# Four settings of the planner that places array visits: entry at a chain's end with five free banks, two sums moved to VectorE, slack for the last inverses

## The chip, the cores and the metric

The kernel runs on one core of one Trainium2 chip. The time is device microseconds of one execution, from the first to the last instruction of that core and what lies around it. The kernel before was timed three times: 385.16, 385.24 and 385.40 us, median 385.24.

## The reference, cut to what matters

Two branches are computed from S = 2048 rows of D = 512 values and mixed by a gate.

```
x = A_q
g = sigmoid((x * gate_w).sum(-1, keepdims=True))
# branch A: a short convolution, a product, a long causal convolution of every channel
k_shift = sum_t k_pad[:, t:t+S, :] * shift_k[:, ks-1-t]      # ks = 4 taps
kv = k_shift * v
y  = irfft(rfft(kv, 2S) * rfft(ssm_k, 2S))[:S] + kv * ssm_D
a  = q * y
# branch B: dense layer, relu, dense layer (512 -> 1792 -> 512)
b  = maximum(x @ w1, 0) @ w2
return g * a + (1 - g) * b
```

All of it is float32. The transform of branch A is done as small matrix products, the dense layers as three products each of a high and a low part (high by high, high by low, low by high).

## The kernel before, in words

TensorE does two kinds of work. **Dense chains** are runs of 128x128 by 512 matmuls that add into one PSUM bank: a chain of the first layer (`mlp1`, lines 412 to 414) has 12 matmuls, a chain of the second (`mlp2`, lines 638 to 640) 15, or 12 in the third era, and a `product` of the last era (lines 496 to 498) 6. The 14 column blocks of the hidden layer are worked in three eras of 5, 5 and 4. In the third era the first layer is computed by a combination of matrix blocks that needs fewer products (`combine`): its tiles are called X, V and Y, and its operands are made by `minus` (line 446) on VectorE.

**Array visits** are runs of 32 small matmuls that use parts of the array side by side (64x32 or 32x64). They carry the convolution:

- `stage1` (line 683): the first step of the two forward transforms, tiles s1x and s1h, in the first 160 us.
- `conv_mid(g, ...)`: the spectral middle, in eight groups g = 0 to 7. Its visit consists of links that follow one another on TensorE: first the inverse of the group two before (`inverse`, line 876, tile iv, four banks), then two rounds f_h and two rounds f_x (line 796), each of two banks. Groups 0 and 1 have no inverse to begin with; two further calls, g = 8 and 9, hold nothing but the inverses of the groups 6 and 7.
- `conv_end` (line 970, tile cy): the last inverse step, four visits after 337 us.

Between the links of a group stands other work: ScalarE copies f_h out (`lower`, line 829, into ha) and the inverse out (line 886, into bv, from where it is stored to HBM as sb); VectorE makes the rest of ha (line 834) and five products with f_x read from PSUM (`mul`, line 842, into p, ha, qa and qb). Then eight additions of 128x512 (`sums`, line 848) fold these into p: the sums 0 and 1 from ha, 2 and 3 from qa, 4 and 5 from qb, 6 and 7 from ha again. GpSimd does them, except those that `DSUM` gives to VectorE: all eight of group 7, and 6 and 7 of group 6. In PSUM all of this shares eight banks with the dense chains (`"cv": 8`): a bank is given back when the engine that reads it has done so, ScalarE for hh, bv and y, VectorE for hl (lines 615 and 519), for y in the second era (line 648) and for f_x (line 842).

The order of every engine's instructions is written out by a planner (`Plan.order`) before the kernel is built. It knows each operation with an estimated duration, a rank, what it depends on and which banks and buffers it takes and gives; it walks through estimated time and starts on every engine the best-ranked operation that is ready. What it writes is a fixed order for each engine; on the chip an instruction then waits for what it needs, and everything behind it on its engine waits too. The planner lets only one of VectorE and GpSimd work on operations that it marks `port` at a time; on the chip nothing holds them apart.

Array links rank ahead of dense work (rank 0 against 1). Without a further rule a visit would start as soon as its operands are there. The rule is `need`: the head of a visit waits until that many of the eight banks are free, unless it has waited 20 us (`PATIENT`). `need` is 6 for the heads of the groups 0 to 7 (`NEEDM`), 4 for the two inverses alone and for `conv_end`. The planner looks at this after every dense operation, and a dense operation is three matmuls, a part of a chain: so a visit may stand within a chain. The flag `ends` marks the last operation of a chain. A dependence that comes from another engine is counted as met a little later than estimated (`SAFE`, 1.0 us for array links).

Of the kernel before, what the change touches and what calls it, by code (L numbers as in the profile page):

```python
# [13 lines left out]
S, D, DFF = 2048, 512, 1792  # L14
# [3 lines left out]
NJ = 32  # L18
# [64 lines left out]
class Plan:  # L83
# [2 lines left out]
    def __init__(self, room):  # L86
        self.room, self.ops, self.turn = dict(room), [], {}

    def add(self, eng, dur, rank, fn, deps=(), take=(), give=(), dma=0, fifo=(), tiles=False, port=False, alt=None, pair=0, soon=False, ends=False, need=0):
        rank = tuple(_flat(rank))  # L90
        op = dict(tiles=tiles, alt=alt, port=port or eng == "POOL" and not dma, eng=eng, dur=dur, rank=rank, fn=fn, take=tuple(take), give=tuple(give), dma=dma, fifo=tuple(fifo),
                  pair=pair, soon=soon, ends=ends or soon, need=need, wait=0, next=[], asked=0.0, n=len(self.ops), rest=(), member=False)
        op["fn"] = fn if alt is None else lambda: fn(op["eng"])
        for d in deps:
            if d is not None:
                d["next"].append(op)
                op["wait"] += 1
        for q in fifo:
            self.turn.setdefault(q, []).append(op["n"])
        self.ops.append(op)  # L100
        return op
# [6 lines left out]
    def order(self):  # L108
        now, seq, events = 0.0, 0, []
# [3 lines left out]
        left, last, out, mode, live, port, live_sums = sum(0 < o["pair"] < 3 for o in self.ops), None, [], False, [], 0.0, False  # L113
# [29 lines left out]
        while True:  # L143
            for eng, ops in ready.items():
                if busy.get(eng, 0.0) > now + 1e-9:
                    continue
                best, summing = None, busy.get("POOL", 0.0) > now + 1e-9 or any(not o["dma"] for o in ready.get("POOL", ()))
                if eng == "POOL":
                    ops = ops + [o for o in ready.get("DVE", ()) if o["alt"] and live_sums]
                late = [o for o in ready.get("DVE", ()) if o["port"] and not o["alt"] and o["asked"] < now - PATIENCE] if eng == "POOL" else ()  # L150
                for op in ops:
                    if eng == "DVE" and op["alt"] and summing and op["asked"] > now - SHARE:
                        continue
                    if op["port"] and (port > now + 1e-9 or late):
                        continue
                    if eng == "PE":
                        if live and op is not live[0]:
                            continue
                        if not live and op["member"]:
                            continue  # L160
                        if op["need"] and not live and op["asked"] > now - PATIENT and op["need"] > sum(o is None or o.get("over", False) for o in line["cv"]):
                            continue
                        if op["pair"] and not live and (left > KEEP or op["pair"] > 2) and op["asked"] > now - LONG[op["pair"] - 1] and not twin(op):
                            continue
                    if best is not None and op["rank"] >= best["rank"]:
                        continue
                    if any(len(line[t]) < op["take"].count(t) or any(o is not None and not o.get("over") for o in line[t][:op["take"].count(t)]) for t in op["take"]):
                        continue
                    if any(self.turn[q][0] != op["n"] for q in op["fifo"]):
                        continue  # L170
                    if op["dma"] and pipe > now + DMA_AHEAD:
                        continue
                    best = op
                if best is None:
                    continue
                op = best
                ready[op["eng"]].remove(op)
                if op["eng"] != eng:
                    op["eng"], op["dur"] = op["alt"]
                live_sums = live_sums or eng == "POOL" and not op["dma"]  # L180
                two = twin(op) if 0 < op["pair"] < 3 and not live else None
                if live and op is live[0]:
                    live.pop(0)
                if op["rest"]:
                    live = list(op["rest"])
                if two:
                    live = [two]
                if eng == "PE":
                    last = op
                    left -= 0 < op["pair"] < 3  # L190
                for t in op["take"]:
                    line[t].pop(0)
                for t in op["give"]:
                    line[t].append(op)
                for q in op["fifo"]:
                    self.turn[q].pop(0)
                op["start"] = now
                if op["port"]:
                    port = now + op["dur"]
                out.append(op)  # L200
                free = now + op["dur"]
                if eng == "PE":
                    if op["tiles"] != mode:
                        free += SWITCH
                    mode = op["tiles"]
                if eng == "PE" and now < PE_COLD:
                    free += op["dur"]
                done = free
                if op["dma"]:
                    pipe = max(pipe, free + DMA_LAG[0]) + op["dma"] / DMA_RATE  # L210
                    done = pipe + DMA_LAG[1]
                op["end"] = done
                busy[eng] = free
                event(free, "free", op)
                event(done + (0 if op["dma"] else LAG.get(eng, 0.0)), "done", op)
            if not events:
                break
            now = events[0][0]
            while events and events[0][0] <= now + 1e-9:
                _, _, what, op = heapq.heappop(events)  # L220
                if what == "wake":
                    continue
                if what == "go":
                    ask(op)
                    continue
                if what == "over":
                    op["over"] = True
                    continue
                if what == "done":
                    late = max([SLOW.get(t, 0) for t in op["give"]], default=0)  # L230
                    if late:
                        event(now + late, "over", op)
                    else:
                        op["over"] = True
                for o in op["next"]:
                    near = o["eng"] == op["eng"] and not op["dma"]
                    if near != (what == "free"):
                        continue
                    o["wait"] -= 1
                    if not o["wait"]:  # L240
                        s = 0 if near else SAFE.get(o["eng"] + str(int(o["rank"][0] != 0)) if o["eng"] == "PE" else o["eng"], 0)
                        if o["member"]:
                            s = 0
                        if o["eng"] == "PE" and not near and now < PE_START and o["rank"][0] == 0:
                            s += 1.5
                        if s:
                            event(now + s, "go", o)
                        else:
                            ask(o)
# [8 lines left out]
def dve_time(n):  # L258
    return n * 0.001042 + 0.12
# [8 lines left out]
def build(tc, wf, xp, qn, kn, vn, hn, dn, sh, gw, w1, w2, cs1, ccf, cci, cib, out):  # L268
# [19 lines left out]
    add = plan.add  # L288
# [490 lines left out]
    def conv_mid(g, gate):  # L779

        rank = (1, 500.0 + 4 * g)
# [2 lines left out]
        chain = []  # L784

        def link(dur, fn, deps, take, give=(), pair=0):
            o = add("PE", dur, (0, rank), fn, (deps if not chain else [chain[-1]]), take, give, tiles=True, pair=pair, need=0 if chain else NEEDM.get(g, 4))
            chain.append(o)
            return o

# [55 lines left out]
        def sums(dst, src, u, n, deps, sign=1, give=(), eng="POOL"):  # L846
            def go():
                (nc.gpsimd if eng == "POOL" else nc.vector).tensor_tensor(planes("p", dst, n), planes("p", dst, n), planes(src, u, n), op=OP.add if sign > 0 else OP.subtract)  # L848

            return add(eng, 0.11 + n * 1.14 if eng == "POOL" else dve_time(n * D), rank, go, deps, (), give, port=True)  # L850

        a = mul(0, 0, "p", 0, 0, 4, ha, give=["cv"], w=("p", 4))
        b = mul(1, 0, "ha", 2, 2, 2, [a])
# [207 lines left out]
DEBUG = None  # L1061
DIRECT = 3,
NEED, PATIENT = 4, 20.0
NEEDM = {g: 6 for g in range(8)}
NE = 4
XW = 512.0
PREP = 42.0, 43.0
SEED = [(2, c) for c in range(4)]
ALT = 0
DSUM = {7: tuple(range(8)), 6: (6, 7)}  # L1070
GATE = 690.0
EARLY = 2, 2
GN = 8
# [77 lines left out]
```

## Time and profile before

| what | value |
|---|---|
| median of three runs | 385.24 us |
| the profiled execution's own time | 384.69 us |
| its span, first to last instruction | 382.9 us |
| TensorE busy | 376.5 us, 98% |
| VectorE busy | 302.3 us, 79% |
| GpSimd busy | 79.1 us, 21% |
| granted TensorE clock | 1.0 throughout |

The profiled execution took 0.55 us less than the median of the others; 1.8 us of its time lie around the span. A matmul's busy time is modelled: dense matmuls are issued every 0.23 us and drawn 0.39 us long, so they overlap in the record, and a pause of TensorE is read from the chain of waits and from the starts, not from the busy sum. In the lists of instructions the first number is the start, the second the duration; in the groups the numbers after the bar are the busy time in us and the mean of one in ns.

### The profile page before, as it was taken

The numbers are of one execution on the slowest core, as the hardware profiler recorded it, in microseconds if no ns is written. First come the engines' busy times: TensorE is split into PE (matmuls) and PEld (weight loads), VectorE is DVE, ScalarE is ACT, GpSimd is POOL, SyncE is SP. The second block draws the span as 40 slices with busy tenths as digits, with TensorE's granted clock in tenths as the row PEclk, the third lists the DMA queues.
The fourth block names the chain that finished last, engine by engine and source line by source line (L and its number), as shares of the span: only waits on it lengthen the run. The fifth ranks groups of instructions, "written<-read, shape, count | busy, mean of one in ns | idle before, by whom it ended". The sixth has DMA issues, their size and how long they took to land.

```text
span 382.9 us, 6634 instructions
## 1 busy us (share of the span) xinstructions
PE 376.5 (98%) x2481; PEld 265.8 (69%) x2481; DVE 302.3 (79%) x389; ACT 169.9 (44%) x311; POOL 79.1 (21%) x63
## 2 busy tenths in 40 slices
PE   9999999999999999999999999999998999999996
PEld 5888866866866886786666465567485877866664
DVE  4699999699599863128868899668999998599863
ACT  5642366176256644523113513452346748464420
POOL 0000000000000000000995758989800000000000
PEclk9999999999999999999999999999999999999999
DMA  8998179777959969699669497899667733959823
GB/s 271 386 299 310 56 277 329 276 256 288 377 163 320 319 210 349 247 309 300 235 221 325 115 364 251 292 314 342 206 199 234 253 111 113 358 196 337 275 98 110
DMA packets 45523, 98.53 MB, mean 257 GB/s; under 512 B 4914, under 2 KB 7730, under 8 KB 45491
## 3 DMA queue, kind: packets, MB, share of 16 engines
q1 hardware_dynamic: 45202, 97.85, 74.4%
q8 instruction: 19, 0.31, 0.3%
q10 hardware_dynamic: 288, 0.26, 0.2%
q14 instruction: 14, 0.11, 0.1%
HBM read 67.68 MB, written 30.41 MB: 256 GB/s over the span
## 4 chain that ended last, share of the span: by engine, by line
PE 98%; DVE 1%; ACT 0%; DVEq 0%; issue 0%
PE m L638 14%; PE m L639 13%; PE m L640 13%; PE m L412 9%; PE m L413 9%; PE m L414 9%; PE iv L876 4%; PE f_h L796 4%; PE f_x L796 4%; PE m L398 3%; PE s1x L683 2%; PE cy L970 2%; PE X L496 2%; PE s1h L683 2%; PE X L497 2%; PE X L498 2%
## 5 line engine op out<-in xcount | busy, mean ns | idle before, releaser
L638 PE MATMUL m<-w1h_h,hh 128*128 128x512 f32 x224 | 89.0, 397 | 0.0
L639 PE MATMUL m<-w1l_l,hh 128*128 128x512 f32 x224 | 87.3, 390 | 0.0
L640 PE MATMUL m<-w1h_h,hl 128*128 128x512 f32 x224 | 87.2, 389 | 0.0
L848 POOL TENSOR_TENSOR p<-p,ha 128x512 f32<-128x512 f32 x26 | 34.0, 1325 | 196.8 <-DVE ha L842 196.3
L612 ACT ACTIVATE hh<-m 128x512 fp32r<-128x512 f32 x40 | 23.6, 599 | 80.6 <-PE m L414 79.8
L638 PEld LDWEIGHTS m<-w1h_h,hh 128*128 128x128 f32 x224 | 42.0, 188 | 20.7 <-ACT ev L688 6.5
L640 PEld LDWEIGHTS m<-w1h_h,hl 128*128 128x128 f32 x224 | 42.0, 188 | 9.0
L615 DVE SCALAR_TENSOR_TENSOR hl<-m,hh 128x512 fp32r<-128x512 f32 x40 | 27.3, 688 | 26.6 <-ACT hh L612 26.6
L639 PEld LDWEIGHTS m<-w1l_l,hh 128*128 128x128 f32 x224 | 42.1, 188 | 8.2
L412 PE MATMUL m<-xh_h,w0h_h 128*128 128x512 f32 x96 | 37.7, 393 | 0.0
L413 PE MATMUL m<-xl_l,w0h_h 128*128 128x512 f32 x96 | 37.4, 389 | 0.0
L414 PE MATMUL m<-xh_h,w0l_l 128*128 128x512 f32 x96 | 37.4, 389 | 0.0
L653 ACT COPY y<-m 128x512 f32<-128x512 f32 x28 | 16.5, 590 | 36.1 <-PE m L640 35.9
L742 DVE TENSOR_TENSOR acc<-acc,tmp 128x1024 f32<-128x1024 f32 x24 | 29.4, 1224 | 0.8
L886 ACT COPY bv<-iv 128x512 f32<-128x512 f32 x32 | 18.3, 598 | 18.7 <-PE iv L876 10.7
L412 PEld LDWEIGHTS m<-xh_h,w0h_h 128*128 128x128 f32 x96 | 18.0, 188 | 6.2 <-ACT bv L886 1.7
L739 DVE TENSOR_TENSOR tmp<-r,sht_sht 128x512 f32<-128x512 f32 x32 | 20.9, 685 | 0.1
L337 DVE TENSOR_TENSOR xl_l<-raw,xh_h 128x512 fp32r<-128x512 f32 x28 | 20.9, 792 | 0.0
L688 ACT COPY ev<-s1x 128x512 f32<-128x512 f32 x32 | 16.4, 600 | 9.7 <-PE s1x L683 9.7
L414 PEld LDWEIGHTS m<-xh_h,w0l_l 128*128 128x128 f32 x96 | 18.0, 188 | 3.8
L848 POOL TENSOR_TENSOR p<-p,qb 128x512 f32<-128x512 f32 x14 | 20.6, 1498 | 0.0
L413 PEld LDWEIGHTS m<-xl_l,w0h_h 128*128 128x128 f32 x96 | 18.0, 188 | 3.6
(149 smaller groups left out, 649.7 us busy)
## 6 DMA issues: line engine op xcount, KB each, us to landing
sa<-ev SPq DMA_DIRECT2D x64, 256.0 KB, 3.0
r_h<-sa SPq DMA_DIRECT2D x16, 512.0 KB, 6.0
r_x<-sa SPq DMA_DIRECT2D x16, 512.0 KB, 7.3
sb<-bv SPq DMA_DIRECT2D x32, 256.0 KB, 3.7
raw<-xp SPq DMA_DIRECT2D x28, 256.0 KB, 4.1
raw<-w SPq DMA_DIRECT2D x22, 256.0 KB, 4.0
r<-kn SPq DMA_DIRECT2D x10, 512.0 KB, 5.3
r<-hn SPq DMA_DIRECT2D x8, 512.0 KB, 4.4
```

Source lines behind the costliest of these rows:

```text
L337: (nc.gpsimd if eng == "POOL" else nc.vector).tensor_tensor(tile_of(lo, tag + "l", dt=F32R, bufs=bufs, p=p), T[key], T[hi].bitcast(F32), o ...
L412: mm(ps, part("h", f, k), T["x", "h", xe, c, k], start=k == 0, stop=False)
L413: mm(ps, part("h", f, k), T["x", "l", xe, c, k], start=False, stop=False)
L414: mm(ps, part("l", f, k), T["x", "h", xe, c, k], start=False, stop=k == 3)
L612: nc.scalar.activation(tile_of(("hh", era, c, f), "hh", dt=F32R, p=mp, bufs=HB), T["m1", era, c, f], AF.Relu)
L615: nc.vector.scalar_tensor_tensor(tile_of(("hl", era, c, f), "hl", dt=F32R, p=mp, bufs=HB), T["m1", era, c, f], 0.0, T["hh", era, c, f].bit ...
L638: mm(ps, T["hh", era, c, f][:, z], T["w", "h", 1, f], start=f == fs[0] and not seeding, stop=False, skip_group_check=True)
L639: mm(ps, T["hh", era, c, f][:, z], T["w", "l", 1, f], start=False, stop=False, skip_group_check=True)
L640: mm(ps, T["hl", era, c, f][:, z], T["w", "h", 1, f], start=False, stop=f == fs[-1], skip_group_check=True)
L742: nc.vector.tensor_tensor(T["acc", c], T["acc", c], T[dst], op=OP.add)
L796: mm(ps[b][32 * j:32 * j + 32, :], T[k("cf")][at, 64 * j + 32 * o:64 * j + 32 * o + 32], T[k("r", t, j // 2)][at, (j % 2) * D:(j % 2 + 1) ...
L848: (nc.gpsimd if eng == "POOL" else nc.vector).tensor_tensor(planes("p", dst, n), planes("p", dst, n), planes(src, u, n), op=OP.add if sign ...
```

## The change

Four things change in the planner's input and rules; no operation is added or taken away.

1. A visit's head (an operation with `need`, outside a running visit) starts only when the operation before it on TensorE was the last of a dense chain (`ends`) or itself an array link (`tiles`), unless it has waited 20 us. With this, `NEEDM` goes from 6 to 5 free banks. The first condition holds for `conv_end` too, whose `need` stays 4.
2. The sums 2 and 3 of group 6 (the seventh), the two from qa, go from GpSimd to VectorE.
3. A new delay `safe` of 2.5 us is added before the planner counts the inverses of the groups 6 and 7 as ready, when their last operand comes from another engine.
4. The planner's estimate for a sum on GpSimd goes from 1.25 to 1.30 us.

```
-    def add(self, eng, dur, rank, fn, ..., ends=False, need=0):
+    def add(self, eng, dur, rank, fn, ..., ends=False, need=0, safe=0):
...
                         if not live and op["member"]:
                             continue
+                        if op["need"] and not live and op["asked"] > now - PATIENT and last and not last["ends"] and not last["tiles"]:
+                            continue
                         if op["need"] and not live and op["asked"] > now - PATIENT and op["need"] > sum(o is None or o.get("over", False) for o in line["cv"]):
                             continue
...
+                        if not near:
+                            s += o["safe"]
                         if s:
                             event(now + s, "go", o)
...
-            o = add("PE", dur, (0, rank), fn, ..., need=0 if chain else NEEDM.get(g, 4))
+            o = add("PE", dur, (0, rank), fn, ..., need=0 if chain else NEEDM.get(g, 4), safe=IVSAFE if g >= NJ // 4 else 0)
...
-            return add(eng, 0.11 + n * 1.14 if eng == "POOL" else dve_time(n * D), rank, go, deps, (), give, port=True)
+            return add(eng, 0.16 + n * 1.14 if eng == "POOL" else dve_time(n * D), rank, go, deps, (), give, port=True)
...
-NEEDM = {g: 6 for g in range(8)}
+IVSAFE = 2.5
+NEEDM = {g: 5 for g in range(8)}
...
-DSUM = {7: tuple(range(8)), 6: (6, 7)}
+DSUM = {7: tuple(range(8)), 6: (2, 3, 6, 7)}
```

More of the change, by code (lines that the diff above doesn't have):

```diff
@@ L87, in __init__, with add @@
         self.room, self.ops, self.turn = dict(room), [], {}
-    def add(self, eng, dur, rank, fn, deps=(), take=(), give=(), dma=0, fifo=(), tiles=False, port=False, alt=None, pair=0, soon=False, ends=False, need=0):
+    def add(self, eng, dur, rank, fn, deps=(), take=(), give=(), dma=0, fifo=(), tiles=False, port=False, alt=None, pair=0, soon=False, ends=False, need=0, safe=0):
         rank = tuple(_flat(rank))
         op = dict(tiles=tiles, alt=alt, port=port or eng == "POOL" and not dma, eng=eng, dur=dur, rank=rank, fn=fn, take=tuple(take), give=tuple(give), dma=dma, fifo=tuple(fifo),
-                  pair=pair, soon=soon, ends=ends or soon, need=need, wait=0, next=[], asked=0.0, n=len(self.ops), rest=(), member=False)
+                  pair=pair, soon=soon, ends=ends or soon, need=need, safe=safe, wait=0, next=[], asked=0.0, n=len(self.ops), rest=(), member=False)
         op["fn"] = fn if alt is None else lambda: fn(op["eng"])
@@ L786, in link @@
         def link(dur, fn, deps, take, give=(), pair=0):
-            o = add("PE", dur, (0, rank), fn, (deps if not chain else [chain[-1]]), take, give, tiles=True, pair=pair, need=0 if chain else NEEDM.get(g, 4))
+            o = add("PE", dur, (0, rank), fn, (deps if not chain else [chain[-1]]), take, give, tiles=True, pair=pair, need=0 if chain else NEEDM.get(g, 4), safe=IVSAFE if g >= NJ // 4 else 0)
             chain.append(o)
```

## The prediction

> **What bounds the kernel now.** I read the page first: which engine is full, and who is on the chain that ended last.
>
> ```profile
> span 382.9 us, 6634 instructions
> ...
> PE 376.5 (98%) x2481; PEld 265.8 (69%) x2481; DVE 302.3 (79%) x389; ACT 169.9 (44%) x311; POOL 79.1 (21%) x63
> ...
> PE 98%; DVE 1%; ACT 0%; DVEq 0%; issue 0%
> ```
>
> TensorE (PE) is the bound from end to end. The change removes no matmul, so it can only win where TensorE pauses, or lose by new pauses. So the second view is the chain of waits in order of time, read visit by visit (start, duration), and the third the timeline of TensorE around the one long pause.
>
> ```profile
> 197.84 1.90 PE iv L876 x32
> 199.75 1.88 PE f_h L796 x32
> 201.62 1.99 PE f_x L796 x32
> ...
> 212.68 1.90 PE iv L876 x32
> ...
> 216.46 2.01 PE f_x L796 x32
> ...
> 227.54 1.90 PE iv L876 x32
> ...
> 231.32 1.99 PE f_x L796 x32
> ...
> 241.01 1.90 PE iv L876 x32
> 242.91 1.88 PE f_h L796 x32
> 244.79 1.72 PE f_x L796 x32
> ...
> 258.67 1.72 PE f_x L796 x32
> ...
> 272.55 1.99 PE f_x L796 x32
> ```
>
> Six visits hold an inverse and a forward part. iv and f_h always take 1.90 and 1.88 us; f_x takes 1.72 in two of them (groups 5 and 6) and about 1.99 in four (groups 2, 3, 4 and 7). These four pauses are 0.27 + 0.29 + 0.27 + 0.27 = 1.10 us.
>
> ```profile
> 289.33 0.39 PE L498 MATMUL X<-xh_h_t,w0l_l_s 128*128 128x512 f32 x1
> 291.54 1.98 PE L876 MATMUL iv<-p,cc 32*64 32x512 f32 x32 [1.82 <-DVE hl L519]
> ```
>
> The inverse of group 6, alone in its visit, stands 1.82 us for VectorE's hl of tile V: it lacks a PSUM bank, not its operand. The groups of waits name no other long one for TensorE's matmuls; what is left is 2.9 us that can be won, 0.8%.
>
> **Why these pauses are there.** First the f_x. I counted the dense matmuls between visits (groups by line, in the windows ahead of the visits of groups 2, 4, 5 and 7).
>
> ```profile
> L412 PE MATMUL m<-xh_h,w0h_h 128*128 128x512 f32 x7 | 2.7, 389 | 0.0
> ...
> L638 PE MATMUL m<-w1h_h,hh 128*128 128x512 f32 x13 | 5.2, 398 | 0.0
> ...
> L412 PE MATMUL m<-xh_h,w0h_h 128*128 128x512 f32 x4 | 1.6, 389 | 0.0
> ...
> L638 PE MATMUL m<-w1h_h,hh 128*128 128x512 f32 x8 | 3.1, 389 | 0.0
> ```
>
> A first-layer chain is four such triples, a second-layer chain five. Ahead of group 2 stand 7 = 4 + 3 triples, ahead of group 4 13 = 5 + 5 + 3, ahead of group 7 8 = 5 + 3: these visits cut a chain open, and all three pause. Group 5 stands after 4, a whole chain, and does not. The open chain keeps its bank through the visit; seven are left for 4 + 4 + 4, so the last f_x round waits for a copy on ScalarE one place further back. Group 3 pauses though it starts at a chain's end; there the queue of ScalarE is the reason:
>
> ```profile
> 213.21 2.17 ACT L334 CAST xh_h<-raw 128x512 fp32r<-128x512 f32 x4
> 215.28 0.58 ACT L886 COPY bv<-iv 128x512 f32<-128x512 f32 x1
> ...
> 229.54 1.07 ACT L886 COPY bv<-iv 128x512 f32<-128x512 f32 x2 [3.55 <-PE iv L876]
> ```
>
> Four casts stand ahead of the first bv, which starts 0.7 us after iv has ended at 214.58 (212.68 + 1.90); behind group 4's iv (227.54 + 1.90) it starts after 0.1.
>
> Then the 1.82 us, from the timelines of VectorE and GpSimd before it.
>
> ```profile
> 269.02 8.18 DVE L446 TENSOR_TENSOR r_b<-r_b,r_b 128x1024 f32<-128x1024 f32 x4
> ...
> 284.16 1.89 DVE L848 TENSOR_TENSOR p<-p,ha 128x512 f32<-128x512 f32 x3
> ...
> 290.71 0.69 DVE L519 SCALAR_TENSOR_TENSOR hl<-V,hh 128x512 fp32r<-128x512 f32 x1
> ```
>
> ```profile
> 268.15 3.51 POOL L848 TENSOR_TENSOR p<-p,qa 128x512 f32<-128x512 f32 x2
> 271.62 4.49 POOL L848 TENSOR_TENSOR p<-p,qb 128x512 f32<-128x512 f32 x2
> ```
>
> ```profile
> L446 DVE TENSOR_TENSOR ha<-ha,ha x2: 1224/1225/1226, 325.1 to 326.3; 128x1024 f32<-128x1024 f32 x2
> ...
> L848 POOL TENSOR_TENSOR p<-p,ha x26: 1284/1297/1730, 182.1 to 266.9; 128x512 f32<-128x512 f32 x26
> ...
> L848 DVE TENSOR_TENSOR p<-p,ha x6: 683/686/689, 284.2 to 305.1; 128x512 f32<-128x512 f32 x6
> ```
>
> Alone, an L446 takes 1.22 us; four would be 4.9. Here they take 8.18: 3.3 us lost while GpSimd's four sums of group 6 run (8.0 us instead of 4 x 1.30 = 5.2). That makes VectorE late for all that follows, hl among it: with 3.3 us less, hl would have been done before the bank was wanted at 289.6. The operand was not late: group 6's own last sum is the second of the three at 284.16, done by 285.4, 4.2 us ahead.
>
> **The change part by part.**
>
> *Entry at a chain's end.* The just ended chain's bank is released within the visit, as in groups 5 and 6. Three cuts healed: 3 x 0.27 = -0.82 us. If copies or casts are in the way, as in group 3, nothing is won there: 0 to -1.10 with group 3. I add half of group 3's, since a visit that moves off the era's last chain leaves the four casts behind: -0.96. For `conv_end` the last visit, at 369 us, moves by at most a few triples; its cover is VectorE's idle time ahead of the last but one output:
>
> ```profile
> 376.42 0.75 DVE L899 SCALAR_TENSOR_TENSOR r<-m,gs_gs,r 128x512 f32<-128x512 f32 x1 [1.75 <-PE m L640]
> ```
>
> VectorE waits 1.75 us there, so a visit two triples later (2 x 3 x 0.23 = 1.4 us) costs nothing; without that cover the tail would grow by up to the shift, one chain's rest of three triples, 2.1 us.
>
> *Five banks instead of six.* Visits may come one chain end earlier than before (group 2 at 195.8 in place of 197.84, by 9 x 0.227 = 2.04 us; likewise groups 4 and 7). TensorE gains nothing by that itself, but the work of VectorE and GpSimd that hangs on a visit starts earlier, and VectorE has room for it in some stretches and none in others (busy time by windows, DVE the third sum):
>
> ```profile
> 192.00:206.00 14.00, 14.00 (x133) 7.96 (x132) 9.64 (x10) 4.33 (x8) 10.35 (x9) 1.00 0.73 238
> 206.00:220.00 14.00, 14.00 (x133) 8.00 (x132) 12.65 (x14) 6.78 (x13) 10.84 (x8) 1.00 0.62 206
> 220.00:235.00 15.00, 15.00 (x138) 8.74 (x137) 14.69 (x14) 4.36 (x8) 10.46 (x8) 1.00 0.91 330
> 235.00:248.00 13.00, 13.00 (x130) 7.65 (x129) 9.62 (x11) 4.21 (x8) 11.22 (x10) 1.00 0.83 266
> 248.00:262.00 14.00, 14.00 (x134) 8.49 (x133) 10.35 (x11) 6.43 (x12) 12.40 (x11) 1.00 0.90 304
> ...
> 276.00:292.00 16.00, 14.18 (x70) 11.31 (x76) 15.90 (x21) 7.30 (x13) 0.11 (x1) 1.00 0.72 225
> ```
>
> The price: one more bank is still in VectorE's hands when the visit begins. iv takes four, f_h needs the fifth and a sixth after 1.90 us and the rest after 2.8. A VectorE that is later than planned by more than that stops TensorE inside the visit. How late it gets in a collision is shown by the splits at 214 us:
>
> ```profile
> 213.95 5.51 DVE L337 TENSOR_TENSOR xl_l<-raw,xh_h 128x512 fp32r<-128x512 f32 x4
> ```
>
> Four splits alone are 4 x 0.69 = 2.8 us, so 2.7 were lost to the two GpSimd sums beside them. A five-bank visit straight behind that pays 2.7 - 1.9 = 0.8; behind the 3.3 of 269 us, 1.4. No such visit is in this trace, so the cost lies between 0 and, for two such hits, 2.2; a shift of the collisions themselves could even save some of it. I take +0.6, nearer to none, because the one inverse that paid did so after the larger collision only.
>
> *Two sums to VectorE.* VectorE gets 2 x 0.686 = 1.37 us more; GpSimd loses 2 x 1.30 = 2.6. Two of the four colliding sums are gone, so I halve the 3.3: VectorE's account is 1.37 - 1.65 = -0.3. Ends: +1.37, if the remaining two still hold all four L446 up, and 1.37 - 3.3 = -1.9, if group 6 comes earlier and nothing collides.
>
> *Slack and estimate.* 2.5 us on an operand that was there 4.2 us early, for a visit that waits for banks: by itself 0. The estimate, 0.05 us for each sum, makes GpSimd's order truer (1.30 measured): 0.
>
> *The pause of 1.82.* VectorE is better off by 0.3 from the sums and by up to 2.04 from group 7's earlier entry: 2.3 against 1.82. That it all arrives is not sure, since VectorE is full from 269 to 292, so I leave 0.3: -1.5.
>
> The sum, against the profiled execution: 384.69 - 0.96 + 0.6 - 1.5 = 382.8 us. The runs' median lies 0.55 above that execution: **383.4 us**.
>
> The Trainium skill bears on the sums. "SBUF — State Buffer", section "SBUF: two separate sides", says that VectorE (with two SBUF inputs) and GpSimd share one pair of ports under an exclusive lock, held for a whole instruction. The stretched L446 and sums above agree in kind. By that rule each sum taken away frees its whole 1.30 us for VectorE, an account of 1.37 - 2.6 = -1.2 in place of my -0.3; the 0.3 us left of the pause would go too: 383.1. Against it speaks "Perfetto Trace Analysis", section "Optimizing Scalar/DVE Operations": moving work between these two might not help because of that port. That is the condition of the first rival below.
>
> **The rivals.**
>
> *The pause stays.* The bank, not the operand, was late, and neither the slack nor the two sums touch a bank. If VectorE's account comes out at +1.37, hl is as late as before even with the earlier visit. Then only the f_x are won, less the new waits: 385.24 - 0.96 + 0.6 = 384.9. For it speaks VectorE's full stretch; against it, that the loss of 3.3 has one visible cause, which shrinks.
>
> *Slower: visits that start too early.* With five banks f_h meets VectorE inside its late stretches at 214 to 219 and 269 to 277. From a lateness of 1.9 us on it decides. Two hits cost 0.8 + 1.4 = 2.2, the pause of 1.82 stays and grows with the extra 1.37 on VectorE, the f_x are won: 385.24 + 2.2 + 1.37 - 0.96 = 387.9 at the worst; with the hit at 269 alone and half of the 1.37, 385.24 + 1.4 + 0.7 - 0.96 = 386.4. For it: the windows at 12.65 of 14 and 14.69 of 15. Against: one visit of six stood behind such a collision before, and waited for ScalarE only.
>
> *All of it goes.* Every pause vanishes and no new one comes: 385.24 - 2.9 = 382.3. A floor: every visit keeps its entry and exit.
>
> **How the numbers follow.** A measurement of this kernel can tell 0.2%, 0.77 us, from no change: 384.47 to 386.01. Forecast with its own spread (382.6 to 384.4) 0.45, all gone 0.13, the pause stays 0.22, slower 0.20. The first two give faster, 0.58; the third lies at 384.9, same, 0.22; the fourth 0.20. The range runs from 382.0 (the floor less 0.3 for the runs' spread) to 386.7, which takes in the slower case but for its worst.
>
> **What would show it.** f_x at 1.72 us in all eight groups confirms the entry at the chain's end; 1.99 in a visit behind a whole chain refutes it. A count of triples ahead of each visit that is a sum of whole chains confirms that the rule acts. The wait of iv for hl gone from TensorE's waits, and the four L446 below 8.18 us, confirm the sums. A new wait of f_h for VectorE, or visits that are not earlier, would prove the five banks wrong. A dense chain that pauses for hl or xl would be a cause that I have not priced, and the forecast would fail by it.

## The result, and the profile after

| what | before | after |
|---|---|---|
| median, lowest and highest of the runs taken side by side | 385.22 us (384.71 to 385.40) | 382.72 us (382.37 to 384.35) |
| profiled execution, its own time | 384.69 us | 382.90 us |
| its span | 382.9 us | 381.1 us |

The ratio is 0.9942, interval 0.9924 to 0.9960: the changed kernel is faster by 0.6%. The granted TensorE clock was 0.998 to 1.0 in every run whose clock is on record here, but for six of the twelve runs of "the change with six banks" below, which show 0.995 to 0.996 and took 386.18 to 387.01 us where the other six took 384.24 to 384.70. Lines behind the change have moved down by 4: L876 is now L880 (iv), L796 is L800 (f_h, f_x), L446 is L450 (`minus`), L848 is L852 (the sums), L519 is L523 (hl of X, V, Y), L638 to L640 are L642 to L644.

The page of the changed kernel, the lines that answer to the first ones of the prediction:

```profile
span 381.1 us, 6637 instructions
...
PE 376.0 (99%) x2481; PEld 266.3 (70%) x2481; DVE 296.5 (78%) x387; ACT 169.9 (45%) x311; POOL 79.4 (21%) x65
...
PE 95%; DVE 1%; DMA 1%; issue 0%; ACT 0%; DVEq 0%
```

TensorE still bounds the kernel and does the same 2481 matmuls. DVE is busy 5.8 us less, although it has two sums more: four splits have gone the other way, to GpSimd, and its other instructions are shorter. The largest group of splits shows it, before (L337) and after (L341):

```profile
L337 DVE TENSOR_TENSOR xl_l<-raw,xh_h 128x512 fp32r<-128x512 f32 x28 | 20.9, 792 | 0.0
```

```profile
L341 DVE TENSOR_TENSOR xl_l<-raw,xh_h 128x512 fp32r<-128x512 f32 x25 | 16.3, 695 | 0.4 <-ACT xh_h L338 0.3
```

A split of this group takes 695 ns in the mean where it took 792. Four of them stood at 214 us beside sums of GpSimd and took 5.51 us; that collision is gone. DMA has a share of the chain that it did not have; that is a new pause, shown below.

The chain of waits of the changed kernel, visit by visit (start, duration):

```profile
195.87 1.90 PE iv L880 x32
...
199.65 1.72 PE f_x L800 x32
...
213.53 1.72 PE f_x L800 x32
...
226.05 1.99 PE f_x L800 x32
...
270.01 1.72 PE f_x L800 x32
...
288.95 1.90 PE iv L880 x32
```

Three of the four f_x pauses are gone (groups 2, 3 and 7); group 4 still has its 0.27 us. The inverse of group 6 follows the dense matmul before it without a wait, 2.6 us earlier than before.

What VectorE did ahead of it, from its timeline:

```profile
263.73 0.68 DVE L852 TENSOR_TENSOR p<-p,qa 128x512 f32<-128x512 f32 x1
...
266.06 1.30 DVE L852 TENSOR_TENSOR p<-p,qa 128x512 f32<-128x512 f32 x1
...
267.88 5.19 DVE L450 TENSOR_TENSOR r_b<-r_b,r_b 128x1024 f32<-128x1024 f32 x3
...
274.19 1.21 DVE L450 TENSOR_TENSOR r_b<-r_b,r_b 128x1024 f32<-128x1024 f32 x1
...
288.13 0.68 DVE L523 SCALAR_TENSOR_TENSOR hl<-V,hh 128x512 fp32r<-128x512 f32 x1
```

and GpSimd beside it:

```profile
266.89 3.85 POOL L852 TENSOR_TENSOR p<-p,qb 128x512 f32<-128x512 f32 x2
```

The four L450 take 5.19 + 1.21 = 6.4 us, where they took 8.18. The last of them ends at 275.4; before, they ended at 277.2. The hl of V that the inverse stood for begins at 288.13 and not at 290.71. The margin is thin: it is done at 288.8, and the inverse starts at 288.9.

One pause is new. The groups of waits name it, and the timeline of ScalarE shows why; the load's row is from the chain of waits:

```profile
PE m L642 <- ACT m L636: 0.6, 1, 0.6
```

```profile
307.67 1.14 ACT L338 CAST xh_h_b<-ha 128x512 fp32r<-128x512 f32 x2 [0.93 <-DMA ha<-xp]
308.72 0.58 ACT L636 COPY m<-y 128x512 f32<-128x512 f32 x1
```

```profile
302.71 4.94 DMA ha<-xp
```

In the third era a chain may begin from a partial sum that ScalarE copies into its bank (m<-y, the seed). In the kernel before, the seed stood ahead of two casts of a freshly loaded block:

```profile
309.30 0.59 ACT L632 COPY m<-y 128x512 f32<-128x512 f32 x1
309.82 1.14 ACT L334 CAST xh_h_b<-ha 128x512 fp32r<-128x512 f32 x2
```

Now it stands behind them, and the casts stand for the load, which lands 4.94 us after its issue. TensorE starts the seeded chain 0.73 us late by the starts of its matmuls.

**Where the time went.** From the first spectral visit to the last dense matmul, by these rows of the chain and the timeline of before, and of after:

```profile
174.48 1.88 PE f_h L796 x32
...
378.71 0.39 PE L640 MATMUL m<-w1h_h,hl 128*128 128x512 f32 x1
```

```profile
175.23 1.88 PE f_h L800 x32
...
376.92 0.39 PE L644 MATMUL m<-w1h_h,hl 128*128 128x512 f32 x1
```

That is 378.71 - 174.48 = 204.23 us before, less 0.68 because the visit now has one triple more ahead of it, so 203.55; and 376.92 - 175.23 = 201.69 after: 1.86 us less. The pauses account for it: -0.82 (three f_x), -1.89 (the inverse, by starts; 1.82 in its row), +0.73 (the seed), together -1.98; the 0.1 us that is left lies behind the seed's pause, where the second matmul of the chain starts 0.34 us after the first (309.36 and 309.69) and dense matmuls otherwise follow at 0.23. The medians differ by 2.5 us. The profiled execution of before lay 0.5 us below its median, that of after 0.2 above; what lies ahead of 175 us varies from one execution to the next: the same changed kernel, profiled again for the last table, had this visit at 175.93.

### The profile page after: what moved, and what is told of

It is laid out like the page before. It is cut to its first block, busy times and chain, and to the rows that moved or that the text cites. A ratio compares the mean times of both kernels' runs of the same rounds, so it can differ in the third digit from the quotient of the medians.

```text
span 381.1 us, 6637 instructions
## 1 busy us (share of the span) xinstructions
PE 376.0 (99%) x2481; PEld 266.3 (70%) x2481; DVE 296.5 (78%) x387; ACT 169.9 (45%) x311; POOL 79.4 (21%) x65
## 4 chain that ended last, share of the span: by engine, by line
PE 95%; DVE 1%; DMA 1%; issue 0%; ACT 0%; DVEq 0%
PE m L642 13%; PE m L644 13%; PE m L643 13%; PE m L416 9%; PE m L417 9%; PE m L418 9%; PE iv L880 4%; PE f_h L800 4%; PE f_x L800 4%; PE m L402 3%; PE s1x L687 2%; PE cy L974 2%; PE X L500 2%; PE s1h L687 2%; PE X L502 2%; PE X L501 2%
## 5 line engine op out<-in xcount | busy, mean ns | idle before, releaser
L642 PE MATMUL m<-w1h_h,hh 128*128 128x512 f32 x224 | 89.0, 397 | 0.6 <-ACT m L636 0.6
L644 PE MATMUL m<-w1h_h,hl 128*128 128x512 f32 x224 | 87.2, 390 | 0.0
L852 POOL TENSOR_TENSOR p<-p,ha 128x512 f32<-128x512 f32 x26 | 33.7, 1312 | 190.5 <-DVE ha L846 190.1
L642 PEld LDWEIGHTS m<-w1h_h,hh 128*128 128x128 f32 x224 | 42.0, 188 | 20.8 <-ACT ev L692 6.5
L644 PEld LDWEIGHTS m<-w1h_h,hl 128*128 128x128 f32 x224 | 42.0, 188 | 9.0
L838 DVE TENSOR_TENSOR ha<-f_h,ha 128x512 f32<-128x512 f32 x16 | 10.6, 689 | 14.0 <-PE f_h L800 13.8
L652 DVE TENSOR_TENSOR y<-m,y 128x512 f32<-128x512 f32 x16 | 10.9, 682 | 12.7 <-PE m L644 12.7
```

The source lines that it names most:

```text
L642: mm(ps, T["hh", era, c, f][:, z], T["w", "h", 1, f], start=f == fs[0] and not seeding, stop=False, skip_group_check=True)
L644: mm(ps, T["hl", era, c, f][:, z], T["w", "h", 1, f], start=False, stop=f == fs[-1], skip_group_check=True)
```

## The experiments

Each ran beside the kernel before on the same chip, five rounds. Two questions: which of the four parts carries the gain, and whether the causes that the prediction named (a bank held by a cut chain; VectorE late because it collides with GpSimd) are the causes.

### The entry rule with five banks, alone

The kernel before, with

```
+   if op["need"] and not live and op["asked"] > now - PATIENT and last and not last["ends"] and not last["tiles"]:
+       continue
...
-NEEDM = {g: 6 for g in range(8)}
+NEEDM = {g: 5 for g in range(8)}
```

> The kernel before with entry at a chain's end and five free banks alone; the sums of group 6 stay on GpSimd, no slack. Theory (the cut chains cost the f_x, an earlier group 7 helps VectorE): f_x at 1.72 us in seven or eight groups, -0.8 to -1.1 us. The four sums still collide with the four L446 (about 8 us), but group 7 enters some 2 us earlier, so the wait of group 6's inverse shrinks from 1.8 to below 1: in all -1.7, 383.5 us. Rival (the two sums are what removes the inverse's wait): the wait stays at 1.5 to 1.9 and only the f_x are won, 384.3 us.

Measured: 382.59 us (382.25 to 384.00), before 385.28; ratio 0.9938 [0.9925, 0.9951]. Its chain of waits:

```profile
226.06 1.99 PE f_x L800 x32
...
270.69 1.99 PE f_x L800 x32
...
289.22 1.95 PE iv L880 x32
```

The whole gain is there without the sums. Two f_x pauses stay, and the inverse of group 6 loses 0.04 us, though the four L450 still take 7.4 us: they start earlier (266.56 against 269.02), since group 6's visit stands at 251.7 in place of 254.9 and VectorE is through with its products sooner.

### The entry rule with six banks, alone

As above, but with the number of before:

```
 NEEDM = {g: 6 for g in range(8)}
```

> The kernel before with entry at a chain's end, six free banks as before. Theory: the same f_x as with five banks, -0.8 to -1.1 us; visits come later than before instead of earlier, so VectorE is as late as before at hl of V and the inverse of group 6 waits 1 to 1.9 us: 384.2 us. Rival (five banks bring nothing, the chain's end does all): no difference from the run with five banks, 383.5 us.

Measured: 383.71 us (383.32 to 384.66), before 385.28; ratio 0.9968 [0.9959, 0.9978]: slower than with five banks by 1.1 us. From its waits, and its chain around 230 us:

```profile
PE f_h L800 <- DVE y L652: 0.6, 1, 0.6
PE iv L880 <- DVE hl L523: 0.4, 1, 0.4
```

```profile
228.88 2.65 DVE w0l_l L341 x2
...
232.19 1.09 PE f_h L800 x16
```

This is the wait that the prediction feared of five banks: f_h stands for a bank in VectorE's hands, since VectorE comes late out of a collision (two splits in 2.65 us instead of 1.28). It came with six, because the visit of group 4 had moved to 228.7, into the collision; with five it starts at 222.2. Of the 1 to 1.9 us expected at the inverse of group 6, 0.5 came; f_h lost 0.8 us instead.

### Five banks, alone

The kernel before, with

```
-NEEDM = {g: 6 for g in range(8)}
+NEEDM = {g: 5 for g in range(8)}
```

> The kernel before with five free banks, visits may still cut a chain open. Theory: five of the six visits now cut a chain (the order written out has them after 8, 10, 10, 11 and 21 triples), each pays 0.3 us or more in f_x, some pay in f_h as well since one bank less is free: f_x and f_h pauses of 1.5 to 3 us in place of 1.1, and the inverse of group 6 stands elsewhere (before the X products), without its 1.8: 384 to 386 us. Rival (earlier visits are good by themselves): below 383.6.

Measured: 383.41 us (383.13 to 383.51), before 385.28; ratio 0.9953 [0.9941, 0.9965]. Its visits again cut chains, five of six, and these five f_x pause; the sixth stands at a chain's end and does not. Groups 2 and 3 of its chain of waits:

```profile
199.34 1.99 PE f_x L798 x32
...
211.46 1.72 PE f_x L798 x32
...
279.53 1.90 PE iv L878 x32
```

Group 3 (nine triples of the first layer ahead: one that ends the cut chain, then two whole chains) runs in 1.72, group 2 (eight, a chain cut) in 1.99. The inverse of group 6 now starts at 279.5, within the second layer's work, and stands for nothing. So the time is that of the rival, below 383.6: the pause of 1.89 us is gone, and five cut chains cost 1.35.

### The two sums, alone

The kernel before, with

```
-DSUM = {7: tuple(range(8)), 6: (6, 7)}
+DSUM = {7: tuple(range(8)), 6: (2, 3, 6, 7)}
```

> The kernel before with the sums 2 and 3 of group 6 on VectorE alone. Theory of the prediction: two colliding GpSimd sums less, the four L446 take 6.5 us in place of 8.2, VectorE does 1.4 us more itself; the wait of group 6's inverse goes from 1.8 to about 1.5 or, if the lock rule holds in full, to 0.6; the f_x stay at 1.99 in four groups: 384.2 to 384.9 us. Rival (the sums alone remove the wait): wait below 0.2, 383.4 us. Rival (moving work between engines that share a port brings nothing): 385.2 us or more.

Measured: 383.28 us (382.88 to 383.96), before 385.28; ratio 0.9951 [0.9939, 0.9963]. VectorE's timeline:

```profile
271.50 3.73 DVE L448 TENSOR_TENSOR r_b<-r_b,r_b 128x1024 f32<-128x1024 f32 x3
...
276.35 1.22 DVE L448 TENSOR_TENSOR r_b<-r_b,r_b 128x1024 f32<-128x1024 f32 x1
```

4.95 us for the four: not half of their loss is gone but all of it, because the two sums left to GpSimd ran at 268.18 to 271.0, ahead of them. But now these meet the two sums that VectorE has taken over:

```profile
267.00 1.65 DVE L850 TENSOR_TENSOR p<-p,qa 128x512 f32<-128x512 f32 x1
...
270.30 1.28 DVE L850 TENSOR_TENSOR p<-p,qa 128x512 f32<-128x512 f32 x1
```

They take 2.93 us where two alone take 1.37, so about half of the collision is left, moved to other instructions. The hl of V starts 2.2 us earlier than before (288.55 against 290.71). About half of that is the collision; the other half is the planner's new order, which puts a product of group 7 (qb, at 292.15 where it was at 286.57) and one sum behind hl, and one split ahead of it. The inverse of group 6 has no pause, as the rival expected; the four f_x of before keep theirs.

### GpSimd held back, the orders as before

To show that the collision is the cause, the kernel before keeps every order, and GpSimd alone is made to wait for the last of the four L446: a tiny extra addition ahead of its sum 2 of group 6 reads one of their outputs.

In `sums`, ahead of the addition:

```
+                if g == 6 and eng == "POOL" and (src, u) == ("qa", 0):
+                    s = tile_of(("scr",), "scr", 8, p=mp)
+                    z = T["xc", 0, "t4"][:, :8]
+                    nc.gpsimd.tensor_tensor(s, z, z, op=OP.add)
```

> The kernel before, every engine's order unchanged, with one small addition of 128x8 on GpSimd ahead of group 6's first qa sum that reads what the last of the four L446 wrote: so GpSimd waits for them and nothing collides there. Theory (the collision makes VectorE late, its lateness makes hl and so the bank late): the four L446 take 4.9 us in place of 8.2, hl of V ends about 3 us earlier, the inverse of group 6 waits less than 0.3 us, the f_x pauses stay: 385.2 - 1.6 = 383.6 us. Rival (the bank is bound otherwise, for instance by ScalarE's hh of V): the wait stays above 1 us, 384.5 to 385.2 us. Rival (GpSimd's sums, now 5 us later, become the operand that is late): a wait for p, 385 us or more.

Measured: 383.17 us (382.81 to 383.74), before 384.96; ratio 0.9958 [0.9946, 0.9971]. GpSimd's timeline, then VectorE's:

```profile
274.44 0.20 POOL L851 TENSOR_TENSOR scr_scr<-r_b 128x8 f32<-128x8 f32 x1 [5.90 <-DVE r_b L446]
274.60 2.55 POOL L852 TENSOR_TENSOR p<-p,qa 128x512 f32<-128x512 f32 x2
277.10 2.55 POOL L852 TENSOR_TENSOR p<-p,qb 128x512 f32<-128x512 f32 x2
```

```profile
269.36 4.99 DVE L446 TENSOR_TENSOR r_b<-r_b,r_b 128x1024 f32<-128x1024 f32 x4
...
288.04 0.69 DVE L519 SCALAR_TENSOR_TENSOR hl<-V,hh 128x512 fp32r<-128x512 f32 x1
```

Nothing was moved off GpSimd, and it idles 5.9 us; the four L446 fall from 8.18 to 4.99 us, hl of V comes 2.7 us earlier, and the pause is gone. TensorE's order is that of the kernel before, matmul by matmul. So VectorE was late because of the collision, and the pause came from that lateness.

### The change without the two sums

The changed kernel, with

```
-DSUM = {7: tuple(range(8)), 6: (2, 3, 6, 7)}
+DSUM = {7: tuple(range(8)), 6: (6, 7)}
```

> The changed kernel with the sums 2 and 3 of group 6 back on GpSimd. Theory: the four L446 meet four sums again, about 8 us in place of 6.3, VectorE is 1 to 2 us later at hl of V, and since the inverse started with a margin of less than 0.1 us behind hl in the changed kernel, its wait comes back with 0.5 to 1.5 us: 383.2 to 384.2 us. Rival (the earlier entry alone has removed the wait): no wait, 382.7 us.

Measured: 383.11 us (382.70 to 384.28), before 384.96; ratio 0.9957 [0.9944, 0.9969]. GpSimd's four sums and the L450 collide as before (7.65 us), yet the inverse of group 6 loses only 0.08 us of the 0.5 to 1.5 expected. What the sums buy inside the change is small: the visit of group 7 pauses 0.57 us in this kernel and not at all in the changed one, and the chain with the seed starts 0.1 us late.

```profile
268.73 2.33 PE f_h L800 x31
```

Of the 0.57, 0.45 are f_h's, 2.33 us long where it is 1.88 in the changed kernel: it stands until 269.97 for a bank that VectorE gives back at 269.93 with its addition into y, late out of the collision. This is the wait that the prediction priced, with five banks; the rest is f_x behind an open chain.

### The change with six banks

The changed kernel, with

```
-NEEDM = {g: 5 for g in range(8)}
+NEEDM = {g: 6 for g in range(8)}
```

> The changed kernel with six free banks. Theory: the visits of groups 2 to 7 come a chain end later (the order written out has group 7 3.6 us later), f_x stays at 1.72 in seven or eight groups, the wait of group 6's inverse is between 0 and 1 us because its own place moves back too: 382.7 to 383.5 us. Rival (five banks are needed): 384 us or more.

Measured: 385.44 us (384.24 to 387.01, 12 runs), before 384.96; ratio 1.0013 [0.9997, 1.0029]. Not 382.7 to 383.5, but the rival's 384 or more. At a granted clock of 1.0 it took 384.24 to 384.70 us, so 0.4 us of the gain is left there; why the clock was lower in the other runs is not shown. A wait from its list, VectorE's timeline at that place, and GpSimd's:

```profile
PE m L642 <- DVE ha L838: 2.0, 1, 2.0
```

```profile
213.81 5.90 DVE L341 TENSOR_TENSOR xl_l<-raw,xh_h 128x512 fp32r<-128x512 f32 x4
```

```profile
212.82 2.98 POOL L852 TENSOR_TENSOR p<-p,qb 128x512 f32<-128x512 f32 x2
215.88 3.28 POOL L852 TENSOR_TENSOR p<-p,ha 128x512 f32<-128x512 f32 x2
```

Four splits that alone take 2.8 us take 5.90 beside four sums; behind them VectorE reads f_h late and gives its bank back late, and the dense chain after group 3's visit cannot begin. In the kernel before, the splits took 5.51 us there and VectorE read f_h hardly sooner (219.38, against 219.63), yet the chain behind that visit began without a wait, in a bank that ScalarE gave back. So it is the collision together with the order in which the banks are handed out that costs the 2 us. The profiled execution took 384.56 us.

### The seed ahead of the casts

The planner's estimate of the load is lengthened until its order puts the seed first; the orders of TensorE, GpSimd and SyncE stay.

In `combine` of the changed kernel:

```
-    raws[nm] = add("SP", ISSUE, -47, go, [...], [...], dma=2 * ROW)
+    raws[nm] = add("SP", ISSUE, -47, go, [...], [...], dma=2.3 * ROW)
```

> The changed kernel with the planner's estimate for four loads of the second combination raised by 15% of their size: this moves on ScalarE one copy (the seed of a bank from y) ahead of two casts that wait for a load, and leaves the order of TensorE, GpSimd and the queues as it is. Theory (the new pause of a dense chain, 0.73 us at 308 us, is the seed standing behind casts whose load lands late): the pause goes, 382.7 - 0.7 = 382.0 us. Rival (the bank of the seed is late anyway): the pause stays, 382.7 us.

Measured: 382.55 us (382.28 to 382.78), before 384.96; ratio 0.9937 [0.9926, 0.9949]. ScalarE's timeline:

```profile
306.96 0.60 ACT L636 COPY m<-y 128x512 f32<-128x512 f32 x1
308.28 1.14 ACT L338 CAST xh_h_b<-ha 128x512 fp32r<-128x512 f32 x2 [0.73 <-DMA ha<-xp]
```

The casts still stand for the load, and nobody stands for them; TensorE's new pause is gone from the profile. The times alone do not show it: 382.55 is nearer to the rival's 382.7 than to 382.0, and the ratio lies within the interval of the changed kernel's first measurement (0.9924 to 0.9960). Nor is the spread of the changed kernel (to 384.35) explained by the seed alone: the two sums alone, whose seed is ahead of the casts, spread from 382.88 to 383.96.

### No visit while a chain is open

Group 4 kept its pause although ten triples, two times five, stand ahead of it. The groups by line, from the end of group 3's visit to the start of group 4's in the changed kernel:

```profile
L642 PE MATMUL m<-w1h_h,hh 128*128 128x512 f32 x6 | 2.3, 389 | 0.0
...
L416 PE MATMUL m<-xh_h,w0h_h 128*128 128x512 f32 x4 | 1.7, 418 | 0.0
```

Four of the first layer, a whole chain, and six of the second: 5 + 1. (The entry rule with five banks alone has such a six ahead of group 4 and of group 7, the two whose f_x pauses there.) Two chains are interleaved there; the last operation before the visit ends one of them, and the other is open, its bank held. So this version of the last kernel counts open chains, one more when a dense operation takes a bank and one less at a chain's end:

```
-   if op["need"] and not live and op["asked"] > now - PATIENT and last and not last["ends"] and not last["tiles"]:
+   if op["need"] and not live and op["asked"] > now - PATIENT and last and (opened > 0 or not last["ends"] and not last["tiles"]):
...
+   if not op["tiles"] and op["rank"][0] == 1 and op["rank"][1] > 0:
+       opened += op["take"].count("cv") - op["ends"]
```

> The changed kernel with the seed moved ahead of the casts, as in the run before, and a stricter rule of entry: a visit starts only when no dense chain is open, not merely when the last operation ended one (group 4's visit entered while another chain, begun one triple before, was open; it moves from after 10 triples to after 14). Theory (an open chain's held bank is what costs f_x 0.27 us): f_x at its short duration in all eight groups, 0.27 us less than with the seed alone, 382.3 us. Rival (group 4 paused for another reason, ScalarE's or VectorE's lateness there): its pause stays or a new one comes in its new place, where the splits of the next chunk lie: 382.6 us or more.

Measured: 382.29 us (381.64 to 382.34), before 384.91; ratio 0.9921 [0.9908, 0.9933]. Group 4 starts after 14 triples:

```profile
225.55 1.90 PE iv L883 x32
...
229.33 1.72 PE f_x L803 x32
```

All f_x take 1.72 now. This version beats both kernels; the changed one on the same chip:

> The changed kernel itself once more, on the same chip, to compare with. 382.7 us; if the seed's pause hangs on when a load lands, it is there in some executions and not in others, so its times scatter by up to 0.7 us more than those of the run beside it.

Measured: 383.55 us (382.70 to 383.94), before 384.91; ratio 0.9957 [0.9945, 0.9969]. In its profile the seed's pause is 1.06 us where it was 0.73: it follows the load, which lands 5.27 us after its issue where it was 4.94.

### Without the slack and the estimate

The changed kernel, with

```
-IVSAFE = 2.5
+IVSAFE = 0
...
-   return add(eng, 0.16 + n * 1.14 if eng == "POOL" else ...)
+   return add(eng, 0.11 + n * 1.14 if eng == "POOL" else ...)
```

> The changed kernel without its parts 3 and 4: the delay before the last two inverses is 0 and the estimate of a sum on GpSimd is 1.25 us again. The delay changes no engine's order, the estimate leaves TensorE's order as it is and moves a few operations of VectorE, ScalarE and GpSimd. Theory (parts 3 and 4 are worth nothing): the visits start where they do in the changed kernel, the inverse of group 6 does not pause, and the ratio to the kernel before is 0.993 to 0.997, like that of the changed kernel. Rival (the estimate carries part of the gain, because it keeps the sums of GpSimd from VectorE's long operations): L450 costs 1 us or more beyond the 6.4 us of the changed kernel, a pause of the inverse of group 6 or of an f_x comes back, and the ratio is 0.998 or more.

Measured: 382.43 us (382.28 to 383.00), before 385.43; ratio 0.9929 [0.9915, 0.9942]. Parts 3 and 4 carry none of the gain. Setting the slack to 0 alters no engine's order; the estimate alters those of VectorE, ScalarE and GpSimd, and here the seed comes first again:

```profile
306.93 0.60 ACT L636 COPY m<-y 128x512 f32<-128x512 f32 x1
307.45 1.14 ACT L338 CAST xh_h_b<-ha 128x512 fp32r<-128x512 f32 x2
```

So inside this change the estimate is what put the casts first. The order alone need not cost anything: with the entry rule and five banks alone, which keeps the old estimate, the casts stand ahead of this seed too (306.99 and 308.04), and no chain waits. The load was issued there at 301.75 us and in the changed kernel at 302.71, with the first visit at the same time in both.

### The pauses against the length of the stretch

For each profiled execution: the pauses between the first spectral visit and the last dense matmul, by the starts of TensorE's instructions, and the length of that stretch as worked out above (0.68 us taken off where 29 triples stand ahead of it instead of 30).

| kernel | f_h and f_x | inverse of group 6 | dense chains, entry | sum | stretch | ratio |
|---|---|---|---|---|---|---|
| before | 1.11 | 1.89 | 0 | 3.00 | 203.55 | 1 |
| entry rule, six banks | 1.09 | 0.50 | 0 | 1.59 | 202.37 | 0.9968 |
| five banks alone | 1.35 | 0 | 0 | 1.35 | 201.89 | 0.9953 |
| two sums alone | 1.11 | 0 | 0 | 1.11 | 201.81 | 0.9951 |
| GpSimd held back | 1.12 | 0 | 0 | 1.12 | 201.71 | 0.9958 |
| entry rule, five banks | 0.54 | 0.04 | 0 | 0.58 | 201.13 | 0.9938 |
| changed | 0.27 | 0 | 0.73 | 1.00 | 201.69 | 0.9942 |
| changed, run again | 0.27 | 0 | 1.06 | 1.33 | 202.02 | 0.9957 |
| changed without the sums | 0.84 | 0.08 | 0 | 0.92 | 201.74 | 0.9957 |
| changed, six banks | 2.72 | 0 | 0 | 2.72 | 203.27 | 1.0013 |
| changed without slack, estimate | 0.27 | 0 | 0.31 | 0.58 | 201.11 | 0.9929 |
| seed first | 0.27 | 0 | 0 | 0.27 | 200.83 | 0.9937 |
| no visit in an open chain | 0 | 0 | 0 | 0 | 200.54 | 0.9921 |

The stretch is 200.54 plus the sum of the pauses, within 0.3 us in every row, and what is over is mostly small gaps in dense chains that the table does not count, such as the 0.1 us behind the seed: TensorE's pauses are what differs between these kernels. In the row "changed, six banks" 2.1 of the 2.72 are the dense chain's wait right behind group 3's f_x. The medians follow the sum less closely (the changed kernel on two chips: 0.9942 and 0.9957), since one profile shows one execution.

## Why the prediction was right, point by point

The forecast, 383.4 us and faster, was right: 382.72. The predicted sum against the profiled execution was -0.96 + 0.6 - 1.5 = -1.86 us, and the profile shows -1.86 in the stretch. That agreement is partly luck: one term had the wrong sign, one was missing, and they cancelled.

- **What bounds the kernel.** Right. "What is left is 2.9 us that can be won": the version without any pause wins 3.0 in the stretch, and its median, 382.29 on a chip where the kernel before took 384.91, is the floor of the fourth case, 382.3.
- **Entry at a chain's end, -0.96.** The mechanism holds: a chain that is left open costs an f_x 0.27 us, in five visits of five with five banks alone, and in group 4 of the changed kernel. -0.82 was measured. Group 3, which the prediction left half open, healed when its visit moved. Group 4, which it counted as healed, did not, and its sign failed with it: "a count of triples ahead of each visit that is a sum of whole chains". Ten can be read as such a sum, yet with interleaved chains the end of one says nothing of the other.
- **Five banks, +0.6.** The term that failed, in size and in sign: with the entry rule, five banks are 1.1 us faster than six. Its mechanism exists, and with five banks too: in the change without the two sums, f_h of group 7 stands 0.45 us for a VectorE that is late out of a collision. But the collisions move with the visits, since each visit starts the sums that collide. The prediction named this ("a shift of the collisions themselves could even save some of it") and priced them as if they stayed in place. In the changed kernel no visit pays for one; with six it loses 2.1 us behind group 3 and 0.3 at group 7.
- **Two sums, VectorE's account -0.3 of -1.9 to +1.37.** The total came out, by luck, and its parts did not. Alone, the sums take the four L446 from 8.18 to 4.95 us, 3.23 less and not 1.65; but they themselves take 2.93 us on VectorE and not 1.37: 2.93 - 3.23 = -0.3. The reasoning "two of the four colliding sums are gone, so I halve" missed that the two left over run earlier and collide with what VectorE does then. In the changed kernel the account is (0.68 + 1.30) - (8.18 - 6.40) = +0.2, so hl is early there through the earlier visits and the new order (with the entry rule and five banks alone it starts at 288.37). The Trainium skill's rule in "SBUF — State Buffer", section "SBUF: two separate sides" (an exclusive lock, held for a whole instruction), gave -1.2 and lay further off, since the sums that were moved met GpSimd's as well. The Trainium skill's "Perfetto Trace Analysis", section "Optimizing Scalar/DVE Operations", says that moving work between these two engines might not help. Here it took 385.28 to 383.28 us, in part through the order that came with it.
- **The pause of 1.82, -1.5.** Right in cause, a little small: -1.89 by starts. It was over-determined. An earlier visit, fewer sums on GpSimd, or GpSimd held back each removes it, so the terms cannot be added: the entry rule with five banks alone has 0.9938, the sums alone 0.9951, both together 0.9942.
- **The rival "the pause stays"** assumed that VectorE's account comes out at +1.37. The account came out at +0.2 and hl was still 2.6 us earlier. The run with GpSimd held back shows why the bank was late: without the collision there is no pause.
- **The rival of visits that start too early** was refuted for this kernel: all f_h take 1.88 us. Its mechanism appears beside it, with five banks without the sums (0.45 us) and with six (0.8 with the entry rule alone, 0.3 in the change).
- **Slack and estimate, 0.** Right for the slack. The estimate is not nothing: in this kernel it turned the order of the seed and the casts, and with the load as late as it was, the seed lost 0.73 us.
- **The end.** `conv_end` costs nothing, as priced; the cover that was named has shrunk to 0.65 us:

```profile
374.63 0.75 DVE L903 SCALAR_TENSOR_TENSOR r<-m,gs_gs,r 128x512 f32<-128x512 f32 x1 [0.65 <-PE m L644]
```

- **Not priced.** "A dense chain that pauses" was named as what would make the forecast fail. It came, 0.73 us, though not for hl or xl: for a seed copy queued behind a cast that stood for a load.

## What to carry to other kernels

When one engine is the bound, add up its pauses by the starts of its instructions: here 3.0 us of pauses were the whole of what any planner setting could win, and the stretch of each variant follows its pauses within 0.3 us. A collision of two engines is not fixed in place: before pricing what stands behind it, follow what the moved work starts, and on which engine. In an order written out ahead, look at every queue for an instruction that waits for a load in front of one that the bound needs; and let "between two chains" mean that no chain is open, not that one has just ended.

## What the runs showed of the hardware

- What a collision costs depends on what meets: four 128x1024 additions on VectorE took 8.18 us beside four sums of GpSimd, 7.4 to 7.65 where four sums met them in another order, 6.4 beside two, and 4.95 to 4.99 with none. An addition of 128x512 on VectorE took 1.28 and 1.65 us beside GpSimd's where it takes 0.69 alone; the sums went from 1.30 us to as much as 2.25 in the collision (4.49 for two).
- The load of the block that is cast at 308 us landed 4.94 us after its issue in one execution of the changed kernel and 5.27 in another, and the pause behind it was 0.73 and 1.06 us. So a fixed order with no slack at a load turns the variation of its landing into time.
- A dense matmul starts 0.23 us after the one before it, but the second one behind a pause or a visit starts 0.34 us after the first, in every kernel here.
